# Loading k and q once per pair of heads h and h+4, on other queues, in a chunked attention kernel with two mixtures of experts

## The chip, the cores and the metric

The program runs on one core of one Trainium2 chip. The metric is the time of one execution in microseconds (us) on the device; lower is better. The core has five engines with a queue of their own each: PE (TensorE, products and weight loads), DVE (VectorE), ACT (ScalarE), POOL (GpSimd) and SP (SyncE, which here only issues transfers), and 16 DMA engines that carry every transfer, whichever queue issued it.

## The reference

Attention in chunks, then a soft mixture of experts, then a second mixture that only changes tokens with a positive score. Cut to what matters here:

```python
# q, k, v: (B=4, H=8, S=768, D=64); mem_k, mem_v: (4, 8, 8, 64)
for c in range(S // 32):                      # chunk of 32 queries
    q_c   = q[:, :, 32*c : 32*c + 32]
    k_ctx = k[:, :, max(0, 32*c - 16) : min(S, 32*c + 40)]   # 16 tokens left, 8 right
    k_full = concat([mem_k, k_ctx]); v_full = concat([mem_v, v_ctx])
    out[chunk] = softmax(q_c @ k_full.T / 8) @ v_full
x = out as (3072 tokens, 512)                 # 8 heads of 64 side by side
logits = x @ phi                              # (512, 32)
slot_input = softmax(logits, over tokens).T @ x           # 32 slots
slot_out[e] = relu(slot_input[e] @ w1[e]) @ w2[e]         # 8 experts, 4 slots each
x = softmax(logits, over slots) @ slot_out
# second mixture: out = x, plus an expert's output for tokens with x @ w_skip > 0
```

## The kernel before

**Units and slots.** The attention goes over 16 units of two heads each (`NU = B * HP`; here a unit is a batch and heads 2hp and 2hp+1), and each unit over two halves of 12 chunks. One half is a slot `n`; there are 32 (`NSLOT`). The order of work is written by hand: the loop `for n in range(NSLOT)` (L589 on) is the program order of every engine. In slot n it issues: `scores(n)`, `probs_T(n-1)`, `x_T(n-2)`, `softmax(n)`, the transposes of k for slot n+3's head (`transpose_k`), `shift_v(n)`, `exps(n)`, the transposes of q (`transpose_q`), the loads of the k and q rows of five slots later (`load_qk(n + 5)`), `values(n-1)`, `normalise(n-1)`, the loads of v for slot n+2 (`load_v`), the logits, and one half-megabyte piece of expert weights (`load_w`, counts in `WPACE`).

**Loads of k and q.** `load_qk(m)` (L206 to L219) loads one head: 100 rows of k (8 tokens of 64 numbers, 2 KB, each; 96 rows and two neighbours on either side) and 96 rows of q, as two transfers. `transpose_k` turns k on PE by four products with the identity (100 rows by 128 columns each), and ACT copies the two halves of the partitions to `ktb`; `transpose_q` does the same with q, to `qT`. There are two buffers `kq`, and two more at the start.

**Loads of v.** A row of `vb` holds two tokens. `load_v` (L224 to L244) issues, per head, 28 rows of 12 blocks of 512 bytes from v and 4 rows of 12 blocks from mem_v. `shift_v` (L277) then copies the second token of each row 32 partitions down, on DVE, two copies of 32 partitions by 768 numbers per slot. There are three buffers `vb` (`NVH`).

**Queues.** All transfers of the attention are issued by SP, in program order, seven per slot: k, q, v, mem_v, v, mem_v, and one weight piece. Eight completion semaphores are used in turn: a transfer is issued when the one eight places earlier has landed (and when its buffer is free).

**Weights.** 44 tiles of half a megabyte hold weight pieces (`NWA + NWB = 30 + 14`); the first 30 are loaded during the attention, the other 34 of the 64 pieces once its buffers are free, while the slot softmax, the experts (`layer1`, `layer2`) and the output rows (`combine`) run.

Of the kernel before, what the change touches and what calls it, by code (L numbers as in the profile page):

```python
# [18 lines left out]
def kernel(  # L19
# [33 lines left out]
    SL = S // 8  # L53
    NBLK = NC + 1
# [7 lines left out]
    NWA, NWB, NWG = 30, 14, 3  # L62
# [3 lines left out]
    WPACE = {**{n: 1 for n in range(24)}, 24: 2, 25: 2, 26: 2}  # L66
# [49 lines left out]
    memkT = keep.tile([P, NU, NMEM], F32, name="memkT")  # L116

    kflat = k.rearrange("b h (p j) d -> (b h p) (j d)", j=8)
    qflat = q.rearrange("b h (p j) d -> (b h p) (j d)", j=8)
    vflat = v.rearrange("b h s d -> (b h s) d")  # L120
# [15 lines left out]
    # in the order in which the last units leave them  # L136
# [9 lines left out]
    # rows of k and q, side by side; their memory holds the transposed row-softmax weights  # L146
    # of the first batches later
    kq = [wa.tile([P, 1024], F32, tag=f"c{i}", name=f"kq{i}") for i in range(2)]
# [35 lines left out]
    def load_small():  # L184
        nc.sync.dma_start(phi_sb, phi.rearrange("(k p) s -> p k s", p=P))
# [5 lines left out]
    # products of no use that keep the tensor engine at its clock while it would wait  # L191
# [6 lines left out]
    def mem_keys():  # L198
        mps = ps_m.tile([P, 512], F32, name="mps", tag="m")
        for f in range(2):  # L200
            nc.tensor.transpose(mps[:, f * P:(f + 1) * P], memn[:, f].rearrange("p j d -> p (j d)"), ident)
        mv = mps[:, :2 * P].rearrange("p (u h n) -> p u h n", h=2, n=NMEM)
        for hh in range(2):
            nc.vector.tensor_copy(memkT[64 * hh:64 * hh + 64], mv[64 * hh:64 * hh + 64, :, hh, :])

    def load_qk(m):  # L206
        u, hh = divmod(m, 2)
        b, hp = divmod(u, HP)
        kn, qn = kq_of(m)
# [11 lines left out]
    def pairs(t, off, rows, blks):  # L221
        return bass.AP(tensor=t.tensor, offset=t.offset + off * D, ap=[[2 * D, rows], [CH * D, blks], [1, 2 * D]])

    def load_v(n):  # L224
        u, z = divmod(n, 2)
        b, hp = divmod(u, HP)
        V = vb[n % NVH]
        for hh in range(2):
            bh = b * H + hp * 2 + hh
            p0 = 64 * hh  # L230
            c = slice(1 + D * hh, 1 + D * hh + 2 * D)
            r0 = bh * S - LC + z * HB * CH
            lo, hi = 0, HB
            if bh == 0 and z == 0:
                lo = 1
                nc.sync.dma_start(V[p0 + LC // 2:p0 + NP, 0:1, c], pairs(v, 0, NP - LC // 2, 1))
            if bh == B * H - 1 and z == 1:
                hi = HB - 1
                nc.sync.dma_start(V[p0:p0 + NP - RC // 2, hi:HB, c], pairs(v, r0 + CH * hi, NP - RC // 2, 1))
            nc.sync.dma_start(V[p0:p0 + NP, lo:hi, c], pairs(v, r0 + CH * lo, NP, hi - lo))  # L240
# [5 lines left out]
    def transpose_k(u, hh):  # L246
        kn = kq_of(2 * u + hh)[0]
        KT = ktb[u % 2]
        kp = ps_tp.tile([P, 4, P], F32, tag="tp", name="kp")
        for j in range(4):  # L250
            nc.tensor.transpose(kp[:, j, :SL + 4], kn[:, j * P:(j + 1) * P], ident[:SL + 4, :SL + 4])  # L251
        o = KT[64 * hh:64 * hh + 64, hh, :, :, 0:CH // 2].rearrange("p a m (r j) -> p a m r j", j=4)
        for a in range(2):
            nc.scalar.copy(  # L254
                o[:, a ^ hh], kp[64 * a:64 * a + 64, :, :SL + 4].rearrange("p j (m r) -> p m r j", r=4)
            )

    def mem_cols(u):
        KT = ktb[u % 2]
        for hh in range(2):  # L260
            pr = slice(64 * hh, 64 * hh + 64)
            for a in range(2):
                (nc.vector if u == 0 else nc.gpsimd).tensor_copy(  # L263
                    KT[pr, hh, a ^ hh, 0:NC, CH // 2:KB],
                    memkT[pr, u, :].rearrange("p (r t) -> p t r", t=2)[:, a].unsqueeze(1).to_broadcast([64, NC, NM]),
                )

    def transpose_q(u, hh):
        qn = kq_of(2 * u + hh)[1]
        qp = ps_tp.tile([P, 4, P], F32, tag="tp", name="qp")  # L270
        for j in range(4):
            nc.tensor.transpose(qp[:, j, :SL], qn[:, j * P:(j + 1) * P], ident[:SL, :SL])  # L272
        o = qTb[u % 2][64 * hh:64 * hh + 64].rearrange("p (s j a) -> p s j a", j=4, a=2)
        for a in range(2):
            (nc.vector.tensor_copy if u == 0 else nc.scalar.copy)(o[:, :, :, a], qp[64 * a:64 * a + 64, :, :SL].rearrange("p j s -> p s j"))  # L275

    def shift_v(n, heads=(0, 1)):  # L277
        V = vb[n % NVH]
        for hh in heads:
            p0, c0 = 64 * hh, 1 + 2 * D * hh  # L280
            nc.vector.tensor_copy(V[p0 + 32:p0 + 64, :, c0:c0 + D], V[p0:p0 + 32, :, D + 1:2 * D + 1])  # L281
# [114 lines left out]
    # slot sums over the batches so far, relative to the largest logit so far  # L396
# [75 lines left out]
    # softmax over the slots, row by row  # L472
# [28 lines left out]
    # row-softmax weights, transposed: high and low parts over four row groups  # L501
    cT, cT_at, crep_t = [], [], {}
# [53 lines left out]
    kq += [wt(NWA - 2), wt(NWA - 1)]  # L556
    make_consts()
    load_qk(0)
    load_mem()
    load_qk(1)  # L560
    load_qk(2)
    warm(ps_m, "m", WARM[0])
    init_kt(0, nc.vector)
    nc.gpsimd.memset(vb[0][0:32, 0, 1:2 * D + 1], 0.0)
# [5 lines left out]
    transpose_k(0, 0)  # L570
    transpose_q(0, 0)
# [20 lines left out]
    for n in range(NSLOT):  # L592
# [13 lines left out]
        if n == 0:  # L606
            transpose_k(1, 0)
            transpose_q(1, 0)
        if n + 3 < NSLOT:
            transpose_k(*divmod(n + 3, 2))  # L610
        shift_v(n, (0, 1) if n < NSLOT - 1 else (0,))
        exps(n)
        step(extra, 4)
        if n + 3 < NSLOT:
            transpose_q(*divmod(n + 3, 2))
            if (n + 3) % 2 == 1:
                mem_cols((n + 3) // 2)
        if 0 < n < NSLOT - 5:
            load_qk(n + 5)
        if n >= 1:  # L620
            values(n - 1)
            normalise(n - 1)
            if n == NSLOT - 1:
                shift_v(n, (1,))
# [20 lines left out]
    cT += [wa.tile([P, 8, P], F32R, tag=f"c{i}", name=f"cT{i}") for i in range(2)]  # L645
# [54 lines left out]
    for kk in range(KD):  # L700
        nc.tensor.matmul(
            sin_ps[:, kk * NS:(kk + 1) * NS], slotp[:, kk * P:(kk + 1) * P], W, start=True, stop=True
        )
# [15 lines left out]
    new_cT()  # L719
# [145 lines left out]
    # rows of the column scores: one copy meets the high part of c, one the low part  # L865
# [49 lines left out]
    # halves of the second columns' experts, between the products of the first columns' rows  # L915
# [188 lines left out]
```

## Time and profile before

| what | value |
|---|---|
| median of three runs (lowest, highest) | 308.61 us (305.58, 311.66) |
| span of the profiled execution, first to last instruction | 304.3 us |
| PE, DVE, ACT, POOL busy, share of the span | 73%, 48%, 41%, 9% |
| granted TensorE clock, mean | 0.811 |
| bytes by DMA, mean rate | 65.98 MB, 217 GB/s |

The profile gives the profiled execution's span and no other time of it, so the runs' median lies 4.3 us above this span. The span has two parts: the attention, to about 238 us, in which the DMA moves 150 to 215 GB/s, and the rest, in which it moves about 350 GB/s until the last rows go out. Busy shares are means over both parts. DMA shares are means over the 16 DMA engines; packets of one engine overlap a little, so a share can be over 1.

### The profile page before, as it was taken

To read this page: it belongs to the slowest core of one execution; us is meant where nothing else is said; L and a number is where in the kernel's file an instruction comes from. 1 tells how busy PE (TensorE), PEld (TensorE's weight loads), DVE (VectorE), ACT (ScalarE), POOL (GpSimd) and SP (SyncE) were. 2 spreads that over 40 slices of the span, in tenths; PEclk is the share of its full clock that TensorE was granted. 3 is DMA by queue.
4 is the path that set the end of the run, shared out by engine and by line. 5 is a ranking of instruction groups with operands and counts; after the bars stand their busy time and mean duration, and the time that the engine had idled before them with its cause. 6 is when DMAs were issued, how large, how long until landed. Compare 5 with 4: busy or idle time off the path is not lost.

```text
span 304.3 us, 7572 instructions
## 1 busy us (share of the span) xinstructions
PE 221.4 (73%) x2934; PEld 161.5 (53%) x2934; DVE 147.4 (48%) x416; ACT 125.3 (41%) x261; POOL 27.8 (9%) x101
## 2 busy tenths in 40 slices
PE   7477767475795795858857885965755989999680
PEld 6366555364574574646655664754644743355450
DVE  6636544444554454445555544545444762333560
ACT  3366444444454554435645445554421410302330
POOL 8211010101001021010010301010101010000000
PEclk9778777969778777757968559689597999999996
DMA  6989887898888879988888788989798899999995
GB/s 176 152 168 186 188 182 181 172 182 187 182 181 196 153 193 189 183 180 188 191 183 195 194 205 190 189 190 204 201 215 179 264 355 348 349 349 349 376 363 168
DMA packets 66044, 65.98 MB, mean 217 GB/s; under 512 B 5088, under 2 KB 51668, under 8 KB 66002
## 3 DMA queue, kind: packets, MB, share of 16 engines
q1 hardware_dynamic: 65570, 63.85, 86.5%
q0 software_dynamic: 432, 1.57, 2.1%
q8 instruction: 25, 0.41, 0.7%
q14 instruction: 17, 0.14, 0.2%
HBM read 59.12 MB, written 6.29 MB: 215 GB/s over the span
## 4 chain that ended last, share of the span: by engine, by line
DMA 75%; PE 16%; DVE 4%; SPq 1%; issue 1%; ACT 0%; DVEq 0%
DMA vb<-in_v_dram 25%; DMA vb<-in_mem_v_dram 19%; DMA w<-in_moe_w_dram 17%; DMA kq<-in_k_dram 8%; DMA kq<-in_q_dram 5%; PE h_ps L731 4%; PE acc L794 3%; PE cp L518 1%; PE o L829 1%; DVE w L836 1%; PE xs L344 1%; PE xtp L379 1%; PE wps L196 1%; PE s_ps L879 1%; DVE x L363 1%
## 5 line engine op out<-in xcount | busy, mean ns | idle before, releaser
L281 DVE COPY vb<-vb 32x768 f32<-32x768 f32 x64 | 35.5, 554 | 95.8 <-DMA vb<-in_mem_v_dram 92.5
L254 ACT COPY ktb<-kp 64x400 f32<-64x400 f32 x64 | 31.2, 487 | 52.1 <-PE kp L251 51.6
L251 PE MATMUL kp<-ident,kq 100*128 100x100 f32 x120 | 21.1, 314 | 31.0 <-DMA kq<-in_k_dram 30.5
L379 PE MATMUL xtp<-ident,x 128*128 128x128 f32 x96 | 19.8, 323 | 32.0 <-DVE x L363 30.0
L297 PE MATMUL s<-ktb,qT 128*32 128x128 f32 x768 | 39.2, 352 | 1.7 <-DVE qT L275 1.7
L344 PE MATMUL xs<-vb,pts 128*32 128x130 f32 x768 | 39.3, 355 | 0.1
L251 PEld LDWEIGHTS kp<-ident,kq 100*128 100x128 f32 x120 | 14.9, 176 | 37.9 <-issue 27.4
L379 PEld LDWEIGHTS xtp<-ident,x 128*128 128x128 f32 x96 | 12.5, 164 | 38.3 <-issue 24.0
L297 PEld LDWEIGHTS s<-ktb,qT 128*32 128x32 f32 x768 | 29.4, 141 | 5.6 <-issue 2.0
L275 ACT COPY qT<-qp 64x384 f32<-64x384 f32 x60 | 30.3, 505 | 1.1
L344 PEld LDWEIGHTS xs<-vb,pts 128*32 128x32 f32 x768 | 25.9, 137 | 6.9 <-issue 3.4
L380 ACT COPY xT<-xtp 128x384 f32<-128x384 f32 x32 | 15.4, 481 | 33.3 <-PE xtp L379 32.9
L332 ACT COPY pts<-pt 128x384 f32<-128x384 f32 x32 | 15.3, 480 | 32.9 <-PE pt L330 32.7
L314 DVE TENSOR_TENSOR pe<-s,mx 128x192 f32<-128x192 f32 (+2 forms) x96 | 22.0, 285 | 5.4 <-PE pt L330 1.2
L263 POOL COPY ktb<-memkT 64x96 f32<-64x96 f32 x60 | 15.0, 278 | 104.0 <-PE s L302 103.2
L330 PE MATMUL pt<-ident,pe 128*128 128x128 f32 x96 | 22.1, 351 | 0.0
L272 PE MATMUL qp<-ident,kq 96*128 96x96 f32 x120 | 20.4, 308 | 1.4 <-DMA kq<-in_q_dram 1.1
L310 DVE TENSOR_REDUCE mx<-s 128x6 f32<-128x384 f32 x32 | 17.6, 549 | 7.2 <-PE s L302 4.2
L363 DVE TENSOR_TENSOR x<-xs,den 128x384 f32<-128x384 f32 x32 | 17.8, 558 | 1.1
L272 PEld LDWEIGHTS qp<-ident,kq 96*128 96x128 f32 x120 | 15.7, 182 | 3.9 <-issue 2.9
L324 ACT ACTIVATE pe<-pe 128x384 f32<-128x384 f32 x32 | 16.8, 524 | 0.7 <-DVE pe L314 0.2
L794 PE MATMUL acc<-w,w 128*32 128x256 f32 x256 | 15.7, 382 | 1.2 <-DMA w<-in_moe_w_dram 1.1
(136 smaller groups left out, 236.6 us busy)
## 6 DMA issues: line engine op xcount, KB each, us to landing
w<-in_moe_w_dram SPq DMA_DIRECT2D x61, 512.0 KB
vb<-in_v_dram SPq DMA_DIRECT2D x62, 168.0 KB
out_dram<-w SPq DMA_DIRECT2D x12, 512.0 KB
kq<-in_q_dram SPq DMA_DIRECT2D x30, 192.0 KB
kq<-in_k_dram SPq DMA_DIRECT2D x28, 200.0 KB
vb<-in_mem_v_dram SPq DMA_DIRECT2D x64, 24.0 KB
w<-in_moe_w_dram POOLq DMA_DIRECT2D x3, 512.0 KB, 9.2
w<-in_k_dram SPq DMA_DIRECT2D x2, 200.0 KB
```

Source lines behind the costliest of these rows:

```text
L251: nc.tensor.transpose(kp[:, j, :SL + 4], kn[:, j * P:(j + 1) * P], ident[:SL + 4, :SL + 4])
L254: nc.scalar.copy(o[:, a ^ hh], kp[64 * a:64 * a + 64, :, :SL + 4].rearrange("p j (m r) -> p m r j", r=4))
L272: nc.tensor.transpose(qp[:, j, :SL], qn[:, j * P:(j + 1) * P], ident[:SL, :SL])
L275: (nc.vector.tensor_copy if u == 0 else nc.scalar.copy)(o[:, :, :, a], qp[64 * a:64 * a + 64, :, :SL].rearrange("p j s -> p s j"))
L281: nc.vector.tensor_copy(V[p0 + 32:p0 + 64, :, c0:c0 + D], V[p0:p0 + 32, :, D + 1:2 * D + 1])
L297: nc.tensor.matmul(o, qT[:, 32 * c:32 * c + 32], KT[:, :, KB * c:KB * c + 32], start=True, stop=not edge)
L314: nc.vector.tensor_tensor(out=pv[:, :, :, o:o + w], in0=sv[:, :, :, i:i + w], in1=mx.unsqueeze(2).to_broadcast([P, TH * 2, 2, w]), op=ALU. ...
L330: nc.tensor.transpose(pt[:, t, :], pe[:, 2 * t:2 * t + 2, :].rearrange("p h c -> p (h c)"), ident)
L344: nc.tensor.matmul(xs[32 * g:32 * g + 32, t], pts[:, t, 32 * g:32 * g + 32], v_cols(V, c - HB * z), start=True, stop=True,)
L363: nc.vector.tensor_tensor(out=x[:, TH * z:TH * z + TH].rearrange("p t (h d) -> p t h d", h=2), in0=xs[:, :, 1:2 * D + 1].rearrange("p t (h ...
L379: nc.tensor.transpose(xtp[:, t, :], x[:, TH * z + t, :], ident)
L794: nc.tensor.matmul(acc[32 * j:32 * j + 32, :cw], hM[kf // 4][:, e, kf % 4, :], w_t["w2", e, ci, kf // 4][:, kf % 4, :], start=(e == 0 and ...
```

## The change

The unit is now a batch and heads h and h+4 instead of two neighbours. One transfer `load_item` brings k of both heads (96 rows, twice 2 KB each), another q of both; k and q alternate, one item per slot, six slots ahead, in three buffers `kq`. The rows of neighbouring heads are not loaded any more: two rows on either side are zeroed at the start or hold older values, which the mask takes out. `transpose_item` turns k as before; for q it uses products with 64 stationary columns, one for each head, that write the upper and the lower half of one bank, so that one copy over 128 partitions takes the place of two over 64. One of a unit's four copies to `ktb` goes to DVE instead of ACT. mem_v is loaded from POOL's queue, weight pieces in the loop from ACT's; SP keeps k, q, v and small loads. `shift_v` runs on POOL. The memory keys are copied to `ktb` by two copies a unit (64 by 192) instead of four (64 by 96). `phi_sb` and the slot inputs (`sin_ps`, eight products of 64 columns instead of four of 128) follow the new order of heads. One weight tile goes to the third `kq` buffer: 29 pieces are loaded in the attention. Core of the diff:

```diff
-    NWA, NWB, NWG = 30, 14, 3
+    NWA, NWB, NWG = 29, 14, 3
-    WPACE = {**{n: 1 for n in range(24)}, 24: 2, 25: 2, 26: 2}
+    WPACE = {**{n: 1 for n in range(25)}, 25: 2, 26: 2}
+    def load_item(i):
+        if i >= 2 * NU:
+            return
+        u, kind = divmod(i, 2)
         b, hp = divmod(u, HP)
-        kn, qn = kq_of(m)
...
-        nc.sync.dma_start(kn[lo:hi], kflat[bh * SL - 2 + lo:bh * SL - 2 + hi, :])
-        nc.sync.dma_start(qn, qflat[bh * SL:(bh + 1) * SL, :])
+        t = kq[i % NKQ].rearrange("p (x c) -> p x c", x=2)
+        p0 = Q0 if kind else K0
+        src = (q if kind else k)[b].rearrange("(x h) (p j) d -> h p x (j d)", x=2, j=8)[hp]
+        nc.sync.dma_start(t[p0:p0 + SL], src)
+    def transpose_item(i):
...
+        for h in range(2):
+            tp = ps_tp.tile([P, 4, P], F32, tag="tp", name="qp" if kind else "kp")
+            if kind:
+                for j in range(4):
+                    c = (2 * j + h) * D
+                    for x in range(2):
+                        nc.tensor.matmul(
+                            tp[D * x:D * x + D, j, :SL], t[:, x, c:c + D], ident[:, Q0:P], start=True, stop=True
+                        )
+                o = qTb[u % 2].rearrange("p (s j a) -> p s j a", j=4, a=2)
+                (nc.vector.tensor_copy if u == 0 else nc.scalar.copy)(
+                    o[:, :, :, h], tp[:, :, :SL].rearrange("p j s -> p s j")
+                )
+                continue
+            rows = SL + 4
+            for j in range(4):
+                nc.tensor.transpose(tp[:, j, :rows], t[:rows, h, j * P:(j + 1) * P], ident[:rows, :rows])
+            o = ktb[u % 2][64 * h:64 * h + 64, h, :, :, 0:CH // 2].rearrange("p a m (r j) -> p a m r j", j=4)
+            for a in range(2):
+                (nc.vector.tensor_copy if h and a else nc.scalar.copy)(
+                    o[:, a ^ h], tp[64 * a:64 * a + 64, :, :rows].rearrange("p j (m r) -> p m r j", r=4)
+                )
...
-            nc.sync.dma_start(
+            nc.gpsimd.dma_start(
                 V[p0 + NP:p0 + 32, :, c],
-                mem_v[b, hp * 2 + hh].rearrange("(r t) d -> r (t d)", t=2).unsqueeze(1).to_broadcast([NM, HB, 2 * D]),
+                mem_v[b, hp + HX * x].rearrange("(r t) d -> r (t d)", t=2).unsqueeze(1).to_broadcast([NM, HB, 2 * D]),
             )
-    def shift_v(n, heads=(0, 1)):
+    def shift_v(n):
         V = vb[n % NVH]
...
-            nc.vector.tensor_copy(V[p0 + 32:p0 + 64, :, c0:c0 + D], V[p0:p0 + 32, :, D + 1:2 * D + 1])
+            nc.gpsimd.tensor_copy(V[p0 + 32:p0 + 64, :, c0:c0 + D], V[p0:p0 + 32, :, D + 1:2 * D + 1])
...
+    nc.vector.memset(kq[0][0:32], 0.0)
+    nc.gpsimd.memset(kq[0][96:P], 0.0)
+    nc.gpsimd.memset(kq[1][0:32], 0.0)
+    load_item(0)
+    load_item(1)
+    load_mem()
     make_consts()
...
-        if n + 3 < NSLOT:
-            transpose_k(*divmod(n + 3, 2))
-        shift_v(n, (0, 1) if n < NSLOT - 1 else (0,))
+        transpose_item(n + 3)
+        if (n + 3) % 2 == 0 and n + 3 < NSLOT:
+            mem_cols((n + 3) // 2)
+        elif n == 0:
+            mem_cols(1)
+        load_item(n + 6)
+        shift_v(n)
         exps(n)
         step(extra, 4)
-        if n + 3 < NSLOT:
-            transpose_q(*divmod(n + 3, 2))
-            if (n + 3) % 2 == 1:
-                mem_cols((n + 3) // 2)
-        if 0 < n < NSLOT - 5:
-            load_qk(n + 5)
...
         for _ in range(WPACE.get(n, 0)):
-            load_w()
+            load_w(nc.scalar)
```

What SP issues for one slot in the middle of the attention, before (line, what, destination and source, shape, and the semaphores it waits for; `DMAHW` are the eight completion semaphores):

```order
L218 DMA kq_107<-in_k_dram 100x512 [waits DMAHW4_49,PE_49]
L219 DMA kq_107<-in_q_dram 96x512 [waits DMAHW5_49,PE_49]
L240 DMA vb_111<-in_v_dram 28x12x128 [waits DMAHW6_49,DVE_49,PE_49]
L241 DMA vb_111<-in_mem_v_dram 4x12x128 [waits DMAHW7_49]
L240 DMA vb_111<-in_v_dram 28x12x128 [waits DMAHW0_49,DVE_49]
L241 DMA vb_111<-in_mem_v_dram 4x12x128 [waits DMAHW1_49]
L551 DMA w_990<-in_moe_w_dram 128x2x512 [waits DMAHW2_49]
```

What SP issues for two slots there now:

```order
L216 DMA kq_109<-in_k_dram 96x2x512 [waits DMAHW7_49,PE_49]
L271 DMA vb_114<-in_v_dram 28x12x128 [waits DMAHW0_49,PE_49,Pool_49]
L271 DMA vb_114<-in_v_dram 28x12x128 [waits DMAHW2_49,Pool_49]
L216 DMA kq_107<-in_q_dram 96x2x512 [waits DMAHW4_49,PE_49]
L271 DMA vb_112<-in_v_dram 28x12x128 [waits DMAHW1_49,DMAHW5_49,PE_49,Pool_49]
L271 DMA vb_112<-in_v_dram 28x12x128 [waits DMAHW6_49,Pool_49]
```

SP's seven transfers per slot became three, and what a v load waits for on the shift is POOL, no longer DVE.

What stands on ACT for two slots now (before there were no transfers on it, and four copies to `qT` and four to `ktb` per unit):

```order
L333 ACTIVATE pe<-pe 128x384 [waits DVE_49,Activation_49]
L554 DMA w_845<-in_moe_w_dram 128x2x512 [waits DMAHW7_49]
L341 COPY pts<-pt 128x384 [waits PE_49,Activation_49]
L389 COPY xT<-xtp 128x384 [waits PE_49,Activation_49]
L234 COPY qT_115<-qp 128x384 [waits PE_49] x2
L333 ACTIVATE pe<-pe 128x384 [waits DVE_49,Activation_49]
L554 DMA w_924<-in_moe_w_dram 128x2x512 [waits DMAHW3_49]
L341 COPY pts<-pt 128x384 [waits PE_49,Activation_49]
L389 COPY xT<-xtp 128x384 [waits PE_49]
L243 COPY ktb_111<-kp 64x25x16 [waits PE_49]
L243 COPY ktb_111<-kp 64x25x16
L243 COPY ktb_111<-kp 64x25x16 [waits PE_49]
```

A weight piece now stands between the exponentials of one slot and the copies of the next, and waits on ACT for one of the eight completion semaphores.

What stands on POOL for two slots now (before, of these, only the copies to `ktb`):

```order
L251 COPY ktb_116<-memkT 64x2x24x4 [waits PE_49,Pool_49]
L251 COPY ktb_116<-memkT 64x2x24x4 [waits Pool_49]
L290 COPY vb_114<-vb_114 32x12x64 [waits DMAHW5_49,DMASW6_49,Pool_49]
L290 COPY vb_114<-vb_114 32x12x64 [waits DMAHW6_49,DMASW7_49,Pool_49]
L281 DMA vb_113<-in_mem_v_dram 4x12x128 [waits PE_49]
L281 DMA vb_113<-in_mem_v_dram 4x12x128
L290 COPY vb_112<-vb_112 32x12x64 [waits DMAHW1_49,DMASW0_49]
L290 COPY vb_112<-vb_112 32x12x64 [waits DMAHW2_49,DMASW1_49]
L281 DMA vb_114<-in_mem_v_dram 4x12x128 [waits PE_49,Pool_49]
L281 DMA vb_114<-in_mem_v_dram 4x12x128 [waits Pool_49]
```

The shift waits there for v (`DMAHW`) and mem_v (`DMASW`, POOL's own completion semaphores), and the mem_v loads of two slots later stand behind it.

## Rows read from the trace of the kernel before

**Rows 1.** Page, span in 40 slices: share of the DMA engines, in tenths.

```profile
DMA  6989887898888879988888788989798899999995
```

**Rows 2.** Windows: us; PE, PEld, DVE, ACT, POOL busy; clock; DMA share; GB/s.

```profile
21.00:228.00 207.00, 147.85 (x2138) 117.10 (x2141) 100.83 (x301) 100.11 (x213) 16.51 (x58) 0.77 0.87 188
245.00:285.00 40.00, 37.47 (x454) 17.06 (x454) 15.71 (x36) 6.17 (x11) 0.82 (x13) 1.00 1.10 351
...
220.00:228.00 8.00, 4.53 (x98) 3.57 (x100) 4.33 (x13) 2.71 (x6) 1.15 (x2) 0.93 1.09 213
```

**Rows 3.** Page, the chain that ended last, by engine.

```profile
DMA 75%; PE 16%; DVE 4%; SPq 1%; issue 1%; ACT 0%; DVEq 0%
```

**Rows 4.** The chain in order of time: start us, us, what.

```profile
69.90 8.52 DMA vb<-in_v_dram
...
78.43 8.00 DMA vb<-in_mem_v_dram
86.45 9.60 DMA w<-in_moe_w_dram
```

**Rows 5.** Waits of SP's queue: who <- for whom: us, times, longest.

```profile
SPq L218 <- DMA w<-in_moe_w_dram: 41.5, 21, 2.8
```

**Rows 6.** Page, DMA issues: count and size of one.

```profile
w<-in_moe_w_dram SPq DMA_DIRECT2D x61, 512.0 KB
vb<-in_v_dram SPq DMA_DIRECT2D x62, 168.0 KB
...
kq<-in_q_dram SPq DMA_DIRECT2D x30, 192.0 KB
kq<-in_k_dram SPq DMA_DIRECT2D x28, 200.0 KB
vb<-in_mem_v_dram SPq DMA_DIRECT2D x64, 24.0 KB
```

**Rows 7.** Waits of the engines: who <- for whom: us, times, longest.

```profile
DVE vb L281 <- DMA vb<-in_mem_v_dram: 92.5, 54, 3.8
...
PE kp L251 <- DMA kq<-in_k_dram: 30.5, 24, 2.6
```

**Rows 8.** Groups by line and shape: busy us, mean ns | idle before.

```profile
L281 DVE COPY vb<-vb 32x768 f32<-32x768 f32 x64 | 35.5, 554 | 95.8 <-DMA vb<-in_mem_v_dram 92.5 <-DMA vb<-in_v_dram 3.0
L254 ACT COPY ktb<-kp 64x400 f32<-64x400 f32 x64 | 31.2, 487 | 52.1 <-PE kp L251 51.6
L275 ACT COPY qT<-qp 64x384 f32<-64x384 f32 x60 | 30.3, 505 | 1.1
...
L263 POOL COPY ktb<-memkT 64x96 f32<-64x96 f32 x60 | 15.0, 278 | 104.0 <-PE s L302 103.2
...
L551 POOL DMA_DIRECT2D w<-in_moe_w_dram x3 | 2.4, 790 | 25.9 <-PE s L302 18.8 <-PE xs L344 7.1
L168 POOL MEMSET vb<- 64x780 f32 x3 | 2.2, 750 | 0.1
...
L263 DVE COPY ktb<-memkT 64x96 f32<-64x96 f32 x4 | 1.7, 776 | 0.1
```

**Rows 9.** Timeline of PE: start us, us, what.

```profile
21.32 0.87 PE L344 MATMUL xs<-vb,pts 128*32 128x130 f32 x24
...
25.46 0.51 PE L272 MATMUL qp<-ident,kq 96*128 96x96 f32 x4
25.90 0.87 PE L344 MATMUL xs<-vb,pts 128*32 128x130 f32 x24
```

**Rows 10.** Line 344 alone: ns min/median/max, first and last start.

```profile
L344 PE MATMUL xs<-vb,pts x768: 272/422/428, 21.3 to 238.1; 128*32 128x130 f32 x192
```

**Rows 11.** Timeline: SP's first load, a weight piece on SP, two on POOL.

```profile
0.74 0.47 SPq L218 DMA_DIRECT2D kq<-in_k_dram  x1
...
100.88 0.39 SPq L551 DMA_DIRECT2D w<-in_moe_w_dram  x1
...
219.55 1.60 POOL L551 DMA_DIRECT2D w<-in_moe_w_dram  x2 [18.80 <-PE s L302]
```

More of the change, by code (lines that the diff above doesn't have):

```diff
@@ L115 @@
     ssum = keep.tile([P, 1], F32, name="ssum")
[L116 to L120, printed above, removed]
+    memkT = keep.tile([P, NU, 2, NM], F32, name="memkT")
     wpools = ctx.enter_context(ExitStack())
@@ L144, in new_v @@
         vb[n % NVH] = bufs.tile([P, HB, VW], F32, name=f"vb{n % NVH}")
-    kq = [wa.tile([P, 1024], F32, tag=f"c{i}", name=f"kq{i}") for i in range(2)]
+    NKQ = 3
+    kq = [wa.tile([P, 1024], F32, tag=f"c{i}", name=f"kq{i}") for i in range(NKQ)]
+    K0, Q0 = 2, P - SL
     new_kt(0)
@@ L221, in pairs @@
-    def pairs(t, off, rows, blks):
-        return bass.AP(tensor=t.tensor, offset=t.offset + off * D, ap=[[2 * D, rows], [CH * D, blks], [1, 2 * D]])
+        mv = mps[:, :2 * P].rearrange("p (b x h r t) -> p x t b h r", x=2, h=HX, t=2, r=NM)
+        for x in range(2):
+            pr = slice(64 * x, 64 * x + 64)
+            for a in range(2):
+                nc.vector.tensor_copy(
+                    memkT[pr, :, a ^ x, :].rearrange("p (b h) r -> p b h r", b=B), mv[pr, x, a]
+                )
@@ L224, in load_v, with mem_cols @@
+    def mem_cols(u):
+        KT = ktb[u % 2]
+        for x in range(2):
+            pr = slice(64 * x, 64 * x + 64)
+            (nc.vector if u == 0 else nc.gpsimd).tensor_copy(
+                KT[pr, x, :, 0:NC, CH // 2:KB],
+                memkT[pr, u].unsqueeze(2).to_broadcast([64, 2, NC, NM]),
+            )
     def load_v(n):
@@ L227, in load_v, with rows @@
         V = vb[n % NVH]
[L228 to L232, printed above, removed]
+        for x in range(2):
+            bh = b * H + hp + HX * x
+            p0, c = 64 * x, slice(1 + D * x, 1 + D * x + 2 * D)
+            t0 = bh * S - LC + z * HB * CH
+            def rows(r0, r1, b0, b1):
+                src = bass.AP(
+                    tensor=v.tensor,
+                    offset=v.offset + (t0 + 2 * r0 + CH * b0) * D,
+                    ap=[[2 * D, r1 - r0], [CH * D, b1 - b0], [1, 2 * D]],
+                )
+                nc.sync.dma_start(V[p0 + r0:p0 + r1, b0:b1, c], src)
             lo, hi = 0, HB
@@ L235, in load_v @@
                 lo = 1
[L236 removed]
+                rows(LC // 2, NP, 0, 1)
             if bh == B * H - 1 and z == 1:
                 hi = HB - 1
[L239 to L241 removed]
+                rows(0, NP - RC // 2, hi, HB)
@@ L242, in load_v @@
+            rows(0, NP, lo, hi)
+            nc.gpsimd.dma_start(
                 V[p0 + NP:p0 + 32, :, c],
-                mem_v[b, hp * 2 + hh].rearrange("(r t) d -> r (t d)", t=2).unsqueeze(1).to_broadcast([NM, HB, 2 * D]),
+                mem_v[b, hp + HX * x].rearrange("(r t) d -> r (t d)", t=2).unsqueeze(1).to_broadcast([NM, HB, 2 * D]),
             )
[L246 to L256, printed above, removed]
@@ L258, in mem_cols @@
-    def mem_cols(u):
-        KT = ktb[u % 2]
-        for hh in range(2):
[L261 to L275, printed above, removed]
@@ L555 @@
     sched.__enter__()
-    kq += [wt(NWA - 2), wt(NWA - 1)]
+    nc.vector.memset(kq[0][0:32], 0.0)
[4 more added lines that the diff above has]
+    load_mem()
     make_consts()
[L558 to L561, printed above, removed]
+    nc.vector.memset(kq[2][0:32], 0.0)
+    nc.vector.memset(kq[2][96:P], 0.0)
+    load_item(2)
     warm(ps_m, "m", WARM[0])
     init_kt(0, nc.vector)
-    nc.gpsimd.memset(vb[0][0:32, 0, 1:2 * D + 1], 0.0)
+    for x in range(2):
+        nc.gpsimd.memset(vb[0][64 * x:64 * x + 32, 0, 1 + D * x:1 + D * x + 2 * D], 0.0)
     for i in range(NVH):
@@ L644 @@
     creps = [c.bitcast(F32R).rearrange("p (t a s) -> p t a s", t=4, a=4) for c in creps]
-    cT += [wa.tile([P, 8, P], F32R, tag=f"c{i}", name=f"cT{i}") for i in range(2)]
+    cT += [wa.tile([P, 8, P], F32R, tag=f"c{i}", name=f"cT{i}") for i in range(NKQ)]
     N1 = NSLOT - 1
@@ L700 @@
     for kk in range(KD):
-        nc.tensor.matmul(
-            sin_ps[:, kk * NS:(kk + 1) * NS], slotp[:, kk * P:(kk + 1) * P], W, start=True, stop=True
-        )
+        for i in range(2):
+            x, h = divmod(2 * kk + i, HX)
+            c = h * P + x * D
+            nc.tensor.matmul(
+                sin_ps[D * i:D * i + D, kk * NS:(kk + 1) * NS], slotp[:, c:c + D], W, start=True, stop=True
+            )
     emask = lp.tile([P, E, NS], F32, name="emask")
@@ L948 @@
     sched.__exit__(None, None, None)
-    free = [i for i in range(NWA + NWB) if i not in cT_at]
+    free = range(NWA + NWB)
     def wf(i):
```

55 lines of the change are left out of this document (18 added, 37 removed).

## The prediction

> **What bounds the kernel now.** I read the chain that ended last first: three quarters of it are transfers [rows 3]. The chain hangs one transfer on the next, each 8 to 9.6 us from issue to landing, and a mem_v load of 24 KB takes as long (8.00 us) as a v load of 168 KB (8.52) or a weight piece of 512 KB (9.60) [rows 4, 6]. A time that does not depend on the size is not the transfer's own; it is the time in the queue behind the seven others in flight. SP confirms it: it waits before its issues for earlier transfers to land, for instance 21 times for a weight piece, 41.5 us in all [rows 5]. The engines wait behind that: DVE stands 92.5 us in front of the shift for mem_v, PE 30.5 us in front of the k transposes [rows 7]. PE is busy for 147.85 of the 207 us between 21 and 228, ACT and DVE for 100 each [rows 2].
>
> So transfers set the pace of the attention. But the DMA engines are not full there: their share is 0.87 at 188 GB/s, while it is 1.10 at 351 GB/s in the rest [rows 2], and the slices show the same step [rows 1]. A queue that always has transfers waiting and engines that idle at the same time go together only when some of the 16 engines have more to do than others, or when eight transfers at a time are too few to fill them. The rate in GB/s is no measure of it, since most v packets are 512 bytes long and the others 1 or 2 KB.
>
> A slot takes (238.1 - 21.3) / 31 = 6.99 us [rows 10]. That compute alone can go faster is seen at the start, where one group of values follows the other after 25.90 - 21.32 = 4.58 us, transposes included [rows 9].
>
> **The change, part by part.** *Transfers.* Per unit, k and q are 392 rows of 2 KB before (200 + 192) and 384 after; v and mem_v keep their packets. One weight piece of 0.524 MB leaves the attention; the window moves 188 GB/s x 207 us = 38.9 MB, so this is 1.3%. The engines' work, share times time, is 0.87 x 207 = 180 us; less 1.3% and about 0.4% for the fewer k rows it is 177 us. What decides is at which share this work is then done. Below: 0.87, as now. Above: 1.10, as in the rest [rows 2]. Between them stands the one stretch of the attention with v loads in flight in which POOL's queue carried weight pieces beside SP's transfers, issued at 219.55 [rows 11]: 220 to 228 us, share 1.09 at 213 GB/s [rows 2]. Two of the causes of idleness are touched: the 100-row loads of k become loads of 96 rows by two, the 4-row loads of mem_v leave SP's queue; the 28-row loads of v stay. And with four transfers instead of seven per slot on the same eight semaphores, two slots' worth may be in flight instead of one. I take 1.0, short of the two high rows, since the v loads remain: 177 us for the window, 30 less. At 0.93 it is 190, 17 less; at 1.10 161, 46 less. A slot is then 6.99 x 177 / 207 = 6.0 us.
>
> The Trainium skill (DMA: Bandwidth & Descriptors, Why a DMA increments its semaphore by 16 and not by 1) says that a transfer runs on the largest number of engines up to 16 that divides its outer dimension, on these queues the lowest-numbered ones. By that rule k runs on 10 engines before and 16 after, v on 14, mem_v on 4, q and weights on 16. Counting bytes, the busiest engine has per slot 32 packets of 2 KB and 72 of 512 bytes before (100 KB) and 28 and 54 to 72 after (83 to 92 KB): an estimate by that page of 0.83 to 0.92 of the window, 17 to 35 us less, around the sum above.
>
> *SP* issues three transfers per slot instead of seven; at 0.39 us for one [rows 11] it was never full. *ACT* loses two of a unit's four qT copies (505 ns) and one of four ktb copies (487 ns) [rows 8], 1.5 us per unit, and gains a 0.39 us issue per slot: per slot 100.11 / 207 x 6.99 = 3.4 us become 3.0. Each issue waits for a semaphore, and the copies of pt, xT, k and q of the next slot stand behind it; PE waits for those. If that wait were SP's longest, 2.8 us [rows 5], ACT would have 5.8 us, still inside a slot of 6.0. I cost it at nothing; without that cover it adds up to 2.8 us x 27 slots.
>
> *DVE* loses the shift (35.5 us) [rows 8], gains 16 copies of about half a us, and no longer stands in front of mem_v; it is not the bound. *PE*: 16 products of 64 columns for 8 of 128 per unit. Four transposes of q take 0.51 us [rows 9], 1.0 per unit; the 24 products of values, four side by side, take 0.87 us, 36 ns each [rows 9]. So the 16 cost between 1.0 us (two halves side by side) and 2.0: at most 16 us in all, under PE's 59 idle us in the window. I take nothing.
>
> *POOL* gets the most. The shift of 768 numbers per partition is not in the trace on POOL: below, a memset of 780 takes 0.75 us; above, a copy of 96 numbers at 278 ns, scaled by eight, gives 2.2 [rows 8]. I take 1.5, nearer to the copy, since it also reads but has a fixed part. A transfer issued on POOL costs 0.79 us (a 512 KB piece) [rows 8]. Per slot: two shifts 3.0, two issues 1.6, half of two copies of 64 x 192 at most 0.5, together 5.1 us (bounds 3.6 and 6.5), against a slot of 6.0. It is hidden, since `values` needs a slot's shift only one slot later; without the cover it is a bound (below).
>
> *Start and end.* The first load, at 0.74 us before [rows 11], waits for memsets of 1024 numbers per partition on DVE and POOL; one of 780 takes 0.75 us [rows 8], so about 1.0 us later. The weight piece that left the attention is loaded in the rest at 351 GB/s: 1.5 us. That stretch is full of transfers (1.10), so all that the attention saves arrives at the end.
>
> Sum: -30 + 1.0 + 1.5 = -27.5 us on a span of 304.3, 276.8. The span is all that the profile gives of its execution; the median of the runs lies 4.3 above it, and I add that: 281.
>
> **The rivals.** *Compute sets the pace after all, later.* If even loads also shorten the packets' own times, slots fall to between 4.6 us [rows 9] and 5.4, by 1.6 to 2.4 x 31 = 50 to 74 us: 237 to 261. Against it: PE's clock is 0.77 on the mean in the window [rows 2], and the 4.58 us are one slot.
>
> *POOL is the bound.* With shifts of 2.2 us it takes 6.5 us per slot: 31 x 0.49 = 15 us less, plus 2.5, 296. For it: nothing shows a copy of this size there.
>
> *Slower: POOL's shift is stretched.* DVE's copy of 64 x 96 at the start took 776 ns beside POOL's memsets, POOL's own of the same shape 278 [rows 8]; two engines can hold each other up. From (6.99 - 1.6 - 0.5) / 2 = 2.45 us per shift on the kernel loses; at 3.0 us a slot takes 8.1, 31 x 1.1 = 34 us more, 345. Against it: the DVE copies between SBUF tiles that run during the loop are just the shifts, and they leave.
>
> The Trainium skill (SBUF — State Buffer, SBUF: two separate sides) says that GpSimd and a VectorE copy from SBUF to SBUF in its fast fp32 form lock each other out, descriptor writing for GpSimd's transfers too. The 776 ns agree; by that rule the loop after the change has few such pairs left, so it lowers this rival's chance.
>
> *The transfers go no faster.* If the share stays 0.87, since the packets and the 16 engines are the same, the window loses 3 us and the ends cost 2.5: 308, no change. Against it: 1.09 in the stretch with a second queue.
>
> The Trainium skill (DMA: Bandwidth & Descriptors, Rules for kernel authors) says that spreading transfers over SP, ACT and GpSimd does not help bandwidth. No run here shows spreading alone; this rule is that rival.
>
> **How the numbers follow.** The runs before spread by 2%, so 2% is about what can be told from no change. Forecast (transfers set the pace at a share of 0.93 to 1.10, 265 to 294): 0.64. Compute earlier: 0.09. POOL at 296: 0.11. No change at 308: 0.09. Slower: 0.07. Faster by over 2% (under 302.4): 0.64 + 0.09 + 0.11 = 0.84; same 0.09; slower 0.07. The predicted time is the forecast's, 281. For 8 in 10 the range leaves out no change and slower (0.16) and the lower part of compute-bound: 260 to 303.
>
> **What would show it.** Right: a DMA share near 1.0 and about 220 GB/s in the attention, slots of about 6.0 us, the last values at about 210 us, a rest as long as before plus 1.5 us. Wrong in the transfers: a share at 0.87 with SP still waiting for landings. Wrong on POOL: shifts over 2 us, POOL busy nearly all of the attention, PE's values waiting for it. Wrong on ACT: ACT's issue of weights waiting for a landing, and PE's transposes for ACT. The forecast falls if a slot stays near 7 us, or if a slot under 5.4 shows that transfers had been no bound of their own.

## The result, and the profile after

| | before | after |
|---|---|---|
| median of four runs (lowest, highest) | 309.95 us (305.58, 311.66) | 282.03 us (280.05, 284.32) |
| span of the profiled execution | 304.3 us | 280.5 us (its own time: 282.38) |
| start of the first and the last product of values | 21.3, 238.1 us | 20.0, 206.8 us |
| slot, (last - first) / 31 | 6.99 us | 6.03 us |
| from the last values to the end of the span | 66.2 us | 73.7 us |

The ratio is 0.93, with a 95% interval of 0.913 to 0.947: faster, by 28 us between the medians, 24 between the two spans, and about 21 by the ratio. Some executions of a kernel take a few per cent longer than its others; the ratios leave those out, so they are not the ratios of the medians. Predicted were 281 us.

The page's slices show the DMA engines' share in tenths; the row of before is in [rows 1]:

```profile
DMA  5899999999999999999999999898589999999983
```

The 7s and 8s of the attention have become 9s; there is one hole, at slices 28 to 30. The same in windows (us; PE, PEld, DVE, ACT, POOL busy; clock; DMA share; GB/s), to be held against [rows 2]:

```profile
21.00:205.00 184.00, 134.09 (x2492) 112.38 (x2484) 81.58 (x267) 77.98 (x172) 93.52 (x148) 0.89 1.03 207
...
220.00:260.00 40.00, 34.89 (x397) 15.00 (x390) 11.14 (x24) 5.64 (x10) 0.00 (x0) 0.96 1.10 351
```

The attention now runs at a DMA share of 1.03 and 207 GB/s, against 0.87 and 188. The granted clock of the window rose from 0.77 to 0.89 with it. Why is not shown: PE is busy for 73% of the window instead of 71%, but in the 100-row kernel below it is busy for 65% only, at a clock of 0.84. Line 353 is the values product (min/median/max ns, first and last start):

```profile
L353 PE MATMUL xs<-vb,pts x768: 272/272/428, 20.0 to 206.8; 128*32 128x130 f32 x192
```

Transfers remain the longest part of the chain that ended last, but 51% of it and no longer 75% [rows 3]:

```profile
DMA 51%; PE 29%; issue 6%; DVE 4%; POOL 4%; SPq 2%; ACT 2%; ACTq 0%; DVEq 0%; POOLq 0%
```

What moved to POOL (line engine op, out<-in, count | busy us, mean ns | idle before):

```profile
L290 POOL COPY vb<-vb 32x768 f32<-32x768 f32 x64 | 53.2, 831 | 84.7 <-DMA vb<-in_v_dram 82.7 <-DMA vb<-in_mem_v_dram 0.6
L281 POOL DMA_DIRECT2D vb<-in_mem_v_dram x64 | 38.6, 608 | 4.5 <-PE xs L353 4.4
...
L251 POOL COPY ktb<-memkT 64x192 f32<-64x192 f32 x30 | 10.2, 339 | 2.7 <-issue 1.3
```

The shift costs 831 ns on POOL against 554 on DVE [rows 8]. The wait in front of it has moved with it: DVE's 92.5 us for mem_v [rows 7] are now POOL's 82.7 for v. The engine that waits is another one; what it waits for is still a transfer.

### The profile page after: what moved, and what is told of

Same layout as the page of the kernel before. It is cut to its first block, busy times and chain, and to the rows that moved or that the text cites. A ratio compares the mean times of both kernels' runs of the same rounds, so it can differ in the third digit from the quotient of the medians.

```text
span 280.5 us, 8277 instructions
## 1 busy us (share of the span) xinstructions
PE 209.6 (75%) x3326; PEld 157.4 (56%) x3326; DVE 123.7 (44%) x368; ACT 100.3 (36%) x215; POOL 115.4 (41%) x202
## 4 chain that ended last, share of the span: by engine, by line
DMA 51%; PE 29%; issue 6%; DVE 4%; POOL 4%; SPq 2%; ACT 2%; ACTq 0%; DVEq 0%; POOLq 0%
DMA w<-in_moe_w_dram 25%; DMA vb<-in_v_dram 22%; PE h_ps L735 5%; PE qp L230 4%; PE xs L353 3%; PE s L306 3%; POOL vb L290 3%; DMA kq<-in_q_dram 2%; PE pt L339 2%; DMA memn<-in_mem_k_dram 2%; PE o L833 2%; SPq L554 1%; PE lg L397 1%; PE xtp L388 1%; PE wps L193 1%
## 5 line engine op out<-in xcount | busy, mean ns | idle before, releaser
L290 POOL COPY vb<-vb 32x768 f32<-32x768 f32 x64 | 53.2, 831 | 84.7 <-DMA vb<-in_v_dram 82.7
L353 PE MATMUL xs<-vb,pts 128*32 128x130 f32 x768 | 32.0, 299 | 29.3 <-POOL vb L290 25.5
L281 POOL DMA_DIRECT2D vb<-in_mem_v_dram x64 | 38.6, 608 | 4.5 <-PE xs L353 4.4
L230 PE MATMUL qp<-ident,kq 128*64 128x96 f32 x512 | 28.9, 270 | 6.2 <-issue 3.9
L370 DVE TENSOR_SCALAR den<-xs 128x6 f32<-128x6 f32 x32 | 5.3, 165 | 58.1 <-PE xs L353 58.0
L230 PEld LDWEIGHTS qp<-ident,kq 128*64 128x64 f32 x512 | 25.1, 152 | 9.3 <-issue 7.5
L243 ACT COPY ktb<-kp 64x400 f32<-64x400 f32 x48 | 23.3, 486 | 18.0 <-PE kp L240 17.4
L234 ACT COPY qT<-qp 128x384 f32<-128x384 f32 x30 | 15.5, 517 | 14.8 <-PE qp L230 13.7
L243 DVE COPY ktb<-kp 64x400 f32<-64x400 f32 x16 | 9.2, 578 | 21.7 <-ACT ktb L243 21.7
L339 PEld LDWEIGHTS pt<-ident,pe 128*128 128x128 f32 x96 | 11.2, 155 | 9.6 <-issue 5.5
```

The costliest lines, as they stand in the source:

```text
L230: nc.tensor.matmul(tp[D * x:D * x + D, j, :SL], t[:, x, c:c + D], ident[:, Q0:P], start=True, stop=True)
L243: (nc.vector.tensor_copy if h and a else nc.scalar.copy)(o[:, a ^ h], tp[64 * a:64 * a + 64, :, :rows].rearrange("p j (m r) -> p m r j", r=4))
L281: nc.gpsimd.dma_start(V[p0 + NP:p0 + 32, :, c], mem_v[b, hp + HX * x].rearrange("(r t) d -> r (t d)", t=2).unsqueeze(1).to_broadcast([NM, ...
L290: nc.gpsimd.tensor_copy(V[p0 + 32:p0 + 64, :, c0:c0 + D], V[p0:p0 + 32, :, D + 1:2 * D + 1])
L339: nc.tensor.transpose(pt[:, t, :], pe[:, 2 * t:2 * t + 2, :].rearrange("p h c -> p (h c)"), ident)
L353: nc.tensor.matmul(xs[32 * g:32 * g + 32, t], pts[:, t, 32 * g:32 * g + 32], v_cols(V, c - HB * z), start=True, stop=True,)
```

## The experiments

Each of the twelve kernels below is compared by its ratio to the kernel before, run beside it on the same chip; on these chips the kernel before took 303.05 to 305.12 us on the median, and the changed kernel, run once more, 281.89, ratio 0.936 (0.928 to 0.944).

Two theories were to be told apart. E: the gain came because some of the 16 DMA engines had more to do than the others, and the new transfers are more even. D: it came because fewer transfers share the same eight semaphores, so that more bytes are in flight.

**100 rows or 112 rows, in the changed kernel.** In `load_item`, R is 100 in one kernel and 112 in the other; rows that the kernel does not use are loaded beside the 96:

```diff
-        nc.sync.dma_start(t[p0:p0 + SL], src)
+        lead = (2 if kind == 0 else R - SL)
+        row = (b * H + hp) * SL - lead
+        src = bass.AP(tensor=a.tensor, offset=a.offset + row * 8 * D, ap=[[8 * D, R], [HX * S * D, 2], [1, 8 * D]])
+        nc.sync.dma_start(t[p0 - lead:p0 - lead + R], src)
```

> The changed kernel, but each k and q item brings 100 rows of both heads instead of 96 (the first and last unit excepted); the extra rows are not used. Theory E (uneven engines: the gain came because k's 100-row transfers left part of the DMA engines idle): the DMA share in the attention falls from 1.03 to about 0.9 and the slot goes from 6.0 back to about 6.9 us, so some 27 us slower, about 309. Theory D (depth: the gain came from fewer transfers on the same eight semaphores, so more bytes in flight): 4% more bytes of k and q, about 1% of all, so 284 at most, share unchanged. The Trainium skill (DMA: Bandwidth & Descriptors, Why a DMA increments its semaphore by 16 and not by 1) puts 100 rows on 10 engines and 96 or 112 on 16; by it the run goes as under E.

> The same with 112 rows instead of 96: 17% more bytes of k and q, three times the extra of the 100-row version. Theory E (uneven engines): the share stays at about 1.03 and only the bytes count, 5% of the attention's work, slot 6.3 us, some 8 us slower, about 290, and clearly faster than the version with 100 rows although it loads more. Theory D (depth): slower than the version with 100 rows by the bytes, about 290 against 284.

Measured: with 100 rows 304.63 us, ratio 0.9985 (0.992 to 1.005), the whole gain gone; with 112 rows, which are more bytes, 291.70 us, ratio 0.962 (0.948 to 0.976). Windows and values of the 100-row kernel:

```profile
21.00:200.00 179.00, 116.79 (x2110) 98.66 (x2110) 67.97 (x225) 66.47 (x146) 79.61 (x128) 0.84 0.90 188
L360 PE MATMUL xs<-vb,pts x768: 271/273/428, 20.9 to 228.2; 128*32 128x130 f32 x192
```

and of the 112-row kernel:

```profile
21.00:200.00 179.00, 125.46 (x2323) 104.90 (x2321) 76.21 (x247) 75.35 (x166) 85.64 (x137) 0.87 1.05 214
L360 PE MATMUL xs<-vb,pts x768: 271/273/428, 21.3 to 212.9; 128*32 128x130 f32 x192
```

Same instructions, same number of transfers, same semaphores; the kernel that loads more is 13 us faster, at a share of 1.05 against 0.90 and slots of 6.18 us against 6.69. For this difference D falls. The DMA engines' idle time hangs on the number of rows of a transfer, as E says. The Trainium skill (DMA: Bandwidth & Descriptors, Why a DMA increments its semaphore by 16 and not by 1) puts 100 rows on 10 engines and 96 or 112 on 16; these two runs agree with it.

No view shows the single engines, but the trace keeps the time of every update of a completion semaphore, and the updates of one transfer can be counted. A load of 96 or 112 rows has 16 updates, one of 100 rows 10, one of v (28 rows) 14, and one of mem_v (4 rows) from SP 4; where there are fewer than 16, one more comes 0.2 us after the issue and is not counted here. Read as one update for each engine that takes part, these are the counts of E. A weight piece has 16. Their times, sorted from first to last and counted from the issue (medians over the pieces issued between 21 and 190 us), tell which engines are behind:

| kernel | early updates of a weight piece | late ones |
|---|---|---|
| before | 12, at 3.7 to 4.5 us | 4, at 5.9 to 9.7 us |
| before, mem_v from POOL (below) | 6, at 4.1 to 5.3 | 10, at 6.8 to 10.9 |
| before, mem_v from POOL and k in 112 rows (below) | 2, at 4.7 to 4.9 | 14, at 6.7 to 11.2 |
| changed | 2, at 4.7 to 5.0 | 14, at 7.4 to 10.6 |
| changed, 100 rows | 6, at 4.3 to 5.0 | 10, at 8.3 to 11.2 |
| changed, 112 rows | 2, at 4.9 to 5.4 | 14, at 8.1 to 11.2 |
| changed, mem_v on SP (below) | 16, at 4.1 to 6.3 | none |
| before, weights from ACT (below) | 16, at 4.1 to 6.6 | none |

The late groups of 4, 10 and 14 are as large as the engine counts of the mem_v, k and v loads, and a group goes when its load is made wider or moved. So E is seen here and not only inferred from the times, in the kernel before as in the changed one. The last two rows are different; they are taken up where these kernels are.

**mem_v on SP again, in the changed kernel.**

```diff
-            nc.gpsimd.dma_start(
+            nc.sync.dma_start(
                 V[p0 + NP:p0 + 32, :, c],
```

> The changed kernel with the mem_v loads issued by SP again. Theory E: these 4-row loads again lie on part of the engines, share about 0.9, slot 6.6 to 6.9, 18 to 27 us slower, 300 to 309. Theory D: six transfers per slot on eight semaphores instead of four, nearly the depth of before (seven), so most of the gain goes: 300 to 309 as well; they differ in that D has SP waiting for landings before most of its issues and all landings of one transfer close together. If neither holds, mem_v's queue is worth nothing: 282.

Measured: 303.20 us, ratio 1.006 (0.998 to 1.014): this alone also takes the whole gain away. Windows, values, the longest wait of an engine, and the two longest of SP's queue:

```profile
21.00:200.00 179.00, 114.06 (x2060) 96.14 (x2060) 69.29 (x225) 67.93 (x151) 49.23 (x75) 0.83 0.86 187
L353 PE MATMUL xs<-vb,pts x768: 272/273/426, 19.3 to 228.3; 128*32 128x130 f32 x192
POOL vb L290 <- DMA vb<-in_mem_v_dram: 117.9, 51, 6.6
SPq L281 <- DMA w<-in_moe_w_dram: 40.9, 12, 8.6
SPq L271 <- DMA w<-in_moe_w_dram: 25.3, 5, 7.6
```

The share is 0.86 as before the change, the slot 6.74 us, and the transfer waited for is mem_v again, the smallest of all at 24 KB. But the cause is not that of the kernel before. The updates of one transfer lie close together (table above), which the expectation had named as the sign of D and not of E; and on the mean 5.3 transfers of SP and ACT are between issue and landing, where the kernel before has 7.9 and the changed one 6.4. SP stands in front of its issues for weight pieces that ACT issues on the same eight semaphores; it does so in the changed kernel too, but there four transfers a slot share them and here six. So the time of this run does not speak for E; what exactly holds SP up here is left open.

**Weights on SP again, in the changed kernel** (`load_w()` for `load_w(nc.scalar)`).

> The changed kernel with the weight pieces of the attention issued by SP instead of ACT. Theories E and D both: the same transfers on the same semaphores, so 282 within 2%. A theory of its own, that a second hardware queue fills the DMA engines better: the share falls from 1.03 toward 0.9 and the time goes to 295 or more.

Measured: 292.47 us, ratio 0.952 (0.937 to 0.968), above the changed kernel's 0.936, but the intervals overlap. E and D had both said 282 within 2%, and this median lies outside. So the second queue may be worth some us; that is not settled here. With mem_v from POOL and k in 96 or 112 rows, weights on SP cost nothing that can be seen (281 us, below).

**The kernel before with one edit each.** First k in 112 rows instead of 100:

```diff
-        nc.sync.dma_start(kn[lo:hi], kflat[bh * SL - 2 + lo:bh * SL - 2 + hi, :])
+        if 0 < bh < B * H - 1:
+            t = kq[m if m in (2, 3) else m % 2]
+            nc.sync.dma_start(t[0:112, 0:512], kflat[bh * SL - 2:bh * SL + 110, :])
```

> The kernel before with one edit: k is loaded in 112 rows per head instead of 100 (12% more bytes of k; the extra rows are not used; first and last head excepted). Theory E (uneven engines): although it loads more, it gains, since the 100-row loads no longer lie on part of the engines; the mem_v loads still do, so only a part: slot 6.99 to about 6.7, ratio to before 0.96 to 0.98. Theory D (depth) and any theory of bytes: 1% slower, ratio 1.00 to 1.01.

Measured: 301.82 us, ratio 0.994 (0.985 to 1.004). It did not lose by its bytes, but it gained less than E had said. Then mem_v from POOL's queue (the same line as above, the other way):

> The kernel before with one edit: mem_v is loaded from POOL's queue. Theory E: the mem_v work leaves the fullest engines, k's stays: slot about 6.5, ratio 0.93 to 0.96. Theory D: five transfers a slot on eight semaphores instead of seven, ratio 0.95 to 0.98. If DVE's shift blocks POOL's descriptors, DVE's wait for mem_v grows and the ratio is 1.0 or more.

Measured: 289.96 us against 304.24 beside it, 0.953 by the medians. The four runs lie at 287.5, 287.6, 292.3 and 296.1 us, and there is no interval. Both edits together:

> The kernel before with both edits, k in 112 rows and mem_v from POOL's queue; nothing else of the change (no merged items, weights on SP, shift on DVE). Theory E: most of the whole change's gain, share 1.0, ratio 0.92 to 0.95. Theory D: no better than mem_v from POOL alone, since k's extra rows only cost.

Measured: 280.99 us, ratio 0.925 (0.906 to 0.945). This is the gain of the whole change, with two edits of some lines. Windows of mem_v from POOL alone:

```profile
21.00:200.00 179.00, 131.90 (x1978) 105.06 (x1978) 95.35 (x284) 94.32 (x201) 49.47 (x114) 0.79 0.96 202
L344 PE MATMUL xs<-vb,pts x768: 272/274/428, 21.8 to 219.1; 128*32 128x130 f32 x192
```

and of both edits:

```profile
21.00:200.00 179.00, 129.45 (x2041) 101.77 (x2034) 98.17 (x293) 97.83 (x208) 51.30 (x117) 0.84 1.08 211
L348 PE MATMUL xs<-vb,pts x768: 271/273/430, 19.4 to 211.7; 128*32 128x130 f32 x192
DVE vb L285 <- DMA vb<-in_v_dram: 66.4, 47, 3.5
```

The share goes from 0.87 to 0.96 with the first and to 1.08 with both, and the slot from 6.99 to 6.36 and 6.20 us. 0.994 times 0.953 would be 0.947; together they give 0.925. The two single factors are too uncertain for the times alone to show more than the product, but it fits E and the table: four engines are late in the kernel before, ten of them (as many as k's) once mem_v is gone, and none stand out from v's 14 once k is wider. D had the pair no better than mem_v alone, and it is 9 us faster. What depth adds to mem_v's own 0.953, with five transfers of SP a slot for seven, was not separated. DVE still waits 66 us in front of the shift, at no cost that the time shows.

Weights from ACT alone, in the kernel before:

> The kernel before with one edit: the weight pieces of the attention are issued by ACT. Theory E: nothing changes on the engines, ratio 0.99 to 1.01. Theory Q (a second hardware queue makes the packets themselves faster, as the 2% loss without it in the changed kernel hints): ratio 0.96 to 0.98. A third: ACT waits for landings and holds PE up, ratio over 1.0.

Measured: 303.23 us, ratio 0.998 (0.988 to 1.007). The time is unchanged, as E says:

```profile
21.00:200.00 179.00, 122.02 (x1826) 99.81 (x1822) 86.65 (x261) 89.02 (x191) 13.54 (x52) 0.79 0.85 186
```

The Trainium skill (DMA: Bandwidth & Descriptors, Rules for kernel authors) says that spreading transfers over the queues does not help bandwidth; for weights from ACT this run's time agrees. Its trace is not that of the kernel before, though: the late group is gone (table above), and 6.1 transfers of SP and ACT are in flight on the mean for 7.9, since SP now waits for weight pieces in front of mem_v. One hindrance went and another came. mem_v from POOL is the exception, 0.953. What differs there is how the load is cut: the trace's packets of POOL's queue have 2 and 4 KB, eight of them for one load of 24 KB, where SP's queue moved 48 of 512 bytes. The larger packets save no engine time: by the trace the packets of one load take 2.4 us together from POOL's queue, and 48 of 512 bytes at the mean of SP's queue as long. That leaves the engines on which the work falls, which the trace does not record for POOL's loads, and depth.

**Both edits, with k in 96 rows** and zeroed neighbours, in the kernel before:

```diff
-        nc.sync.dma_start(kn[lo:hi], kflat[bh * SL - 2 + lo:bh * SL - 2 + hi, :])
+        nc.sync.dma_start(kn[2:SL + 2], kflat[bh * SL:(bh + 1) * SL, :])
...
+        e_.memset(t[0:2, 0:512], 0.0)
+        e_.memset(t[96:P, 0:512], 0.0)
```

> The kernel before with two edits: k is loaded in 96 rows per head (the two rows on either side zeroed once at the start, as the changed kernel has it) and mem_v from POOL's queue. Theory E: at least as fast as with 112 rows, since 14% of k's bytes are gone: slot 6.0 to 6.1, ratio 0.91 to 0.92, at or below the whole change. If the whole change's other parts (merged items, weights on ACT, shift on POOL, q by 64 columns) carry a gain of their own, it stays above the changed kernel by that.

Measured: 281.19 us, ratio 0.920 (0.908 to 0.931), beside 281.89 and 0.936 of the changed kernel. So merged items, weights on ACT, the shift on POOL and q's 64-column products bring nothing together that can be measured beside these two edits.

**The shift on DVE again, in the changed kernel** (`nc.vector.tensor_copy` in `shift_v`).

> The changed kernel with the shift of v's tokens on DVE again. If the shift on POOL matters (DVE no longer stands in front of v's landing, so the normalisation is earlier), the time rises by 1 to 3%. If the transfers alone set the pace, it stays within 1% of the changed kernel.

Measured: 281.82 us, ratio 0.926 (0.914 to 0.938), the changed kernel's time, although the waits are those of a kernel in which DVE holds up the normalisation:

```profile
PE xtp L388 <- DVE x L372: 50.4, 23, 6.5
...
DVE vb L290 <- DMA vb<-in_v_dram: 43.0, 29, 4.3
```

This is a good pair of rows to remember: 50 us of PE waiting for DVE, and removing the cause brings no time. In the changed kernel PE waits 25.5 us for POOL's shift instead, which waits for the same v.

**Weights later, in the changed kernel.** The hole in the DMA slices, in windows of the changed kernel:

```profile
190.00:195.00 5.00, 3.29 (x40) 2.80 (x42) 0.91 (x4) 2.27 (x5) 1.80 (x3) 0.66 1.03 166
195.00:200.00 5.00, 4.66 (x117) 3.90 (x118) 3.16 (x11) 1.48 (x3) 4.80 (x8) 1.00 0.46 105
200.00:205.00 5.00, 4.24 (x87) 3.29 (x86) 3.48 (x13) 2.86 (x6) 4.32 (x6) 1.00 0.70 180
```

```diff
-    WPACE = {**{n: 1 for n in range(25)}, 25: 2, 26: 2}
+    WPACE = {n: 1 for n in range(2, 31)}
```

> The changed kernel with its 29 weight pieces one per slot in slots 2 to 30 instead of one in slots 0 to 24 and two in 25 and 26. In the changed kernel the DMA share falls to 0.46 between 195 and 200 us and 0.70 between 200 and 205: all pieces are in, and the last v loads wait for values. If that hole costs time at the end, four pieces moved into it save up to 5 us, ratio 0.91 to 0.92; if the end of the attention is set by the last v loads themselves, or the late pieces delay them, no change or some us slower.

Measured: 277.88 us (277.02 to 280.89), ratio 0.923 (0.916 to 0.931); the changed kernel beside it 281.89 (279.93 to 285.71):

> The changed kernel unchanged, beside the three others on the same chip: ratio 0.92 to 0.94.

The hole is gone:

```profile
195.00:200.00 5.00, 3.83 (x83) 3.01 (x83) 2.54 (x11) 2.17 (x5) 3.15 (x5) 1.00 1.09 199
200.00:205.00 5.00, 1.08 (x12) 0.47 (x11) 1.26 (x4) 0.96 (x2) 1.42 (x2) 0.86 1.05 276
```

This is the fastest kernel of the study by its median, 4 us under the changed one; five of its six runs lie under the lowest of the changed kernel, though the intervals of the two ratios overlap a little.

## Why the prediction was right, point by point

**The bound.** Right: transfers on unevenly loaded engines set the pace. The window's work was taken as conserved (177 us) and divided by a share of 1.0; the share came out at 1.03, the slot at 6.03 us for 6.0, the rate at 207 GB/s for 220. That the slot fits so well is partly luck: the work was not conserved. Share times slot was to fall from 6.08 to 6.0 us and rose to 6.2; the higher share makes up for it. Two causes of the idleness were named, the 100-row loads and the 4-row loads. Undoing either takes the whole gain back, and in the kernel before removing both gives it; but mem_v put back on SP in the changed kernel costs by another cause, as said there. A third way to explain it, eight transfers being too few in flight, was left standing beside them in the prediction. It does not explain what the number of rows does; for mem_v's queue it is not excluded as a part.

**The size of each cause** was not in the sum. The prediction's count by bytes took 8 KB per slot off the busiest engine for k and up to 9 KB for mem_v, about equal; alone, k's rows gave 0.6%, not clear of nothing, and mem_v 4.7%. With mem_v moved, k's rows gave another 9 us.

**Start.** The first load was 1.3 us later, not 1.0, and it cost nothing: the first values came at 20.0 us, 1.3 earlier than before. SP's first load, to be held against [rows 11]:

```profile
2.01 0.40 SPq L216 DMA_DIRECT2D kq<-in_k_dram  x1
```

**The attention** ended 31.3 us earlier by the start of its last values (238.1 to 206.8); the sum had 29 (-30 + 1.0).

**The rest is the term that was mis-sized.** Predicted was 1.5 us more for one weight piece; measured are 7.5 (73.7 for 66.2). The step that failed is "That stretch is full of transfers (1.10), so all that the attention saves arrives at the end." Its head is not full: after the change the share is 0.46, 0.70 and 0.78 in the three stretches of 5 us from 195 to 210 us. SP's first late weight issue stood at 227.98 us before the change, 10.1 us before the start of the last values; now it stands at 201.84, only 5.0 us before it. From that issue to the end, 76.3 us became 78.7: 2.4 more, where 1.5 were counted. The other 5 us are the hole: all 29 pieces were in, and SP's last loads of v waited 9.0 us for products of values to free their buffers. The kernel with later weights gives 4 of them back.

**From span to time.** 4.3 us were added to the span; the profiled execution took 1.9 more than its span. The sum by spans was 27.5 us less, measured are 23.8. So the predicted 281 is nearer to the measured 282 than the steps behind it are: a rest 6 us too short and an offset 2.4 us too long, with 2 us more gained in the attention. That the number came within 1 us is luck: the misses cancel.

**POOL.** Taken were two shifts of 1.5 us, two issues of 0.79 and 0.5 for the copies to ktb, 5.1 us per slot; measured 0.83 twice, 0.60 twice and 0.34 once per slot, 3.2 us, under the lower bound of 3.6. That the shift lies under the memset's row plus a little says which row was the near one: 831 ns for 768 numbers beside 750 for a memset of 780 [rows 8]. Scaling the 96-number copy by eight scaled its fixed part too. The rivals on POOL fell with it; the shift was never stretched, 824 to 837 ns over 64.

**ACT.** Per slot 77.98 / 184 x 6.03 = 2.6 us busy; ACT's own waits show no landing that it stood for in the loop, though one weight issue is on the chain, at 30 us. The wait showed up on SP: 79.3 us in front of its issues for weight pieces, and five pieces of the attention are on the chain. That it costs nothing is borne out by the times only: the kernel before with k in 112 rows, mem_v from POOL and weights on SP takes 280.99 us.

**PE.** The 32 parts of a unit's q products took 1.50 to 2.36 us where the chain shows them, for 1.0 to 2.0 taken; they are on the chain for 4% of the span, so they were not wholly covered, though they had been taken so.

## What to carry to other kernels

When a kernel waits for transfers while the DMA share is well under what the same trace shows elsewhere, look at the outer counts of the transfers before their bytes or queues: 112 rows loaded faster than 100. A small broadcast load on four rows can set the pace of everything (24 KB; in the kernel before its queue alone was worth 14 of 304 us). The updates of one wide transfer's semaphore tell whether some engines are behind: two groups of times with a gap say yes, and how many. And when the loop gets shorter, look at the seam behind it: what was prefetched in its last rounds may no longer reach.

## What the runs showed of the hardware that was not expected

- Loads with 17% more bytes of k and q were 13 us faster than loads with 4% more: 112 rows against 100, share 1.05 against 0.90.
- The completion semaphore of a load from SP has 16 updates with 96 or 112 rows, 10 with 100, 14 with 28 and 4 with 4; the times of a weight piece's 16 updates show how many engines are behind (4 in the kernel before, which had its last at 9.7 us where the first 12 came by 4.5).
- A load of 4 rows by 12 blocks of 512 bytes that goes out from POOL's queue is moved in eight packets of 2 and 4 KB instead of 48; its issue took 0.60 us there.
- POOL's copy takes about as long as its memset of that length: 831 ns for 768 numbers (32 partitions) beside 750 for 780; a copy of 192 (64 partitions) took 339.
- The larger packets of POOL's queue saved no engine time: 2.4 us of packets for a load of 24 KB, as from SP.
